# Attention and a Mish layer on one core: Mish written in bf16 steps with one reciprocal for eight denominators, and the exponential's VectorE share raised to 50 sets at a constant pace

## The chip, the cores and the metric

One Trainium2 chip, of which the program uses one core. The metric is the time of one execution in device microseconds (us). Three runs of the kernel before took 901.83, 902.10 and 903.09 us; their median is 902.1 us. In this text PE or TensorE is the matrix engine, ACT or ScalarE the engine of activations, DVE or VectorE the vector engine, POOL or GpSimd the fourth compute engine, SP the queue that issues most transfers.

## The reference

Two branches on the same input `x` (2048 rows of 640, bf16) are mixed by a gate per row:

```python
g = sigmoid((x * gate_w).sum(-1))                    # one gate per row
qkv = x @ wqkv                                       # 32 heads of 20 columns each
p = softmax(q @ k.T * 20**-0.5)                      # per head, 2048 x 2048
a = (p @ v) @ wo
h = x @ w1 + b1                                      # 2048 x 1536
sp = log1p(exp(-abs(h))) + max(h, 0)
b = (h * tanh(sp)) @ w2                              # Mish, then the second matrix
out = g * a + (1 - g) * b
```

With n = e^h (e^h + 2), Mish is h * n / (n + 2); the kernel computes it so. The softmax has 32 x 2048 x 2048 exponentials, 1,048,576 in each of the 128 partitions.

## The kernel before

**Attention.** The heads are taken four at a time (a "pair" `p`, 0 to 7; the name is the code's) and the queries 512 at a time (`qc`, 0 to 3). A (p, qc) is a *group*; there are 32. A group has 16 *sets*, one for each 128 keys, and a set has four *blocks*, one per head: 128 keys x 512 queries of scores. L1150 multiplies `kT` (32 rows of each of the four heads) by `qT` into a PSUM tile `Sp`; L1165 takes the exponential of a whole tile into `E`; L1225 multiplies `E` by the values `VA`, four heads beside each other, into the accumulator `acc`. The values carry a column of ones, so a row of `acc` is the softmax's sum. At the end of a group `normalise` (L1180 to L1211, all on VectorE) turns `acc` round (L1185), inverts the sums, scales, and turns it back into a 128x512 `cell` (L1202).

The score tiles alternate between three blocks (tag S0) and two blocks (tag S1), one buffer each, so scores of iteration i+2 need the tile of iteration i back. One *iteration* is one tile. There are 819.

**The exponential on two engines.** Some sets go to VectorE. In an iteration with a three-block tile, ACT then reads only two blocks, and VectorE reads the third (L794 in `jv_read`) into one slot of `E_dve` (a ring of three buffers). After four such reads a set is complete, and seven further steps (L810 to L832 in `jv_steps`) work the exponential out in integer and fp16 arithmetic, 2048 elements per partition each. L1225 then uses it with `VB`, a scaled copy of the values. `JV_SETS` says how many sets of a group are VectorE's, `JV_START` and `blocks` at which point of the run (in groups) each read is due: groups 1 to 31 have one and two sets in turn, 47 in all, and the reads of group G begin 0.9 of a group before it (other offsets for groups 1, 25 and 32).

**The Mish branch.** `h_chain` multiplies `x` by `w1` (L660), VectorE adds the bias (L670); for each pair of 512-wide pieces `mish_steps` (L579 to L645) issues one ACT exponential into a float32 tile `e` (L589) and then eleven VectorE instructions. Before, these are, each on 1024 elements unless said otherwise: n (L596, float32 to float32), the clip and + 2 (L599, float32 to fp16 `d`), products of two denominators (L603, 512, float32 out), of four (L608, 256), two reciprocals (L609, 128 each), back to two (L612, 512), back to one (L618), n times the inverse (L626, with float32 input), and two products with h (L632, 512 each). `b_chain` multiplies the result by `w2` (L693), scales it by 1 - g (L705).

**The end.** The first six pairs' cells go to memory and come back when a query chunk's turn comes (`fetch`); pairs 6 and 7 keep theirs. When a query chunk has all eight, `wo_chain` multiplies by `wo` (L739), and L756 adds the two branches and stores the rows. For the last chunk this is done without pair 7 into `R`; the very end adds pair 7's part (L1408, L1421).

**What orders the work.** The program is written out by hand, in one order per engine, by a planner in the kernel's own code. It keeps a clock per engine (`T`) with a cost for each instruction. `pump` puts pieces of projection, Mish and output matmuls (the chains, with start and due iteration) between an iteration's scores and the next; where nothing is due it puts in a filling multiplication of a constant tile (L1090), to keep TensorE active. `steps` and `run_slow` place the VectorE steps of the Mish pairs, the seven steps of a set and the rest of `normalise` into the gaps that VectorE's clock has before the next read. `wo_sb` is cleared by eight VectorE memsets (L1350) during group 16, before its load.

An iteration with a three-block tile gets a read by VectorE when the next one is due:

```python
x = None
far = G + (pos - unit_at[(G, 0)]) / (4.0 * (NS - JV_SETS.get(G, 0)))
if n == 3 and blocks and blocks[0][0] <= far:
    ...
    n = 2
```

Of the kernel before, what the change touches and what calls it, by code (L numbers as in the profile page):

```python
# [2 lines left out]

# [147 lines left out]
def kernel(  # L151
# [12 lines left out]
    nc = tc.nc  # L164
# [8 lines left out]
    QC = 512  # L173
    NQC = S // QC
    NU = QC // P
    NQ = H // 4
# [2 lines left out]
    Q_SCALE = 512.0 * float(DH) ** -0.5 / LN2  # L179
    WIDTHS = (3, 2)  # L180

    JV_TWO = (*range(2, 31, 2), 31)
    JV_SETS = {G: 2 if G in JV_TWO else 1 for G in range(1, 32)}
    JV_RING = 3
    JV_AHEAD = 0.9
    JV_BIAS = 32
    N_CAP = 16382.0
    NCELL = 40
    MLP_FROM, MLP_TO = 10, 1
    CELLS_KEPT = 2  # L190

# [111 lines left out]


    groups = [(p, qc) for p in range(NQ - 2) for qc in range(NQC)]
    groups += [(p, qc) for qc in range(NQC) for p in (NQ - 2, NQ - 1)]
    first = {}
    for G, (p, qc) in enumerate(groups):
        first.setdefault(p, G)


    units = []
# [6 lines left out]
    JV_START = {G: G - JV_AHEAD for G in range(34)}  # L319
    JV_START.update({1: 0.95, 25: 24.85, 32: 31.1})  # L320
    blocks = deque(
        (JV_START[G] + b * min(1.0, JV_START[G + 1] - JV_START[G]) / n, G, k, c)
        for G in JV_SETS
        for n in (4 * JV_SETS[G],)
        for b, (k, c) in enumerate((k, c) for k in range(JV_SETS[G]) for c in range(4))
    )
# [32 lines left out]
    def it_at(G, j=0):  # L359
        return it_of[unit_at[(G, j)]] if G < len(groups) else NI  # L360
# [218 lines left out]
    def mish_steps(m, c):  # L579


        h = h_of.pop((m, c))
        mish_free[0] = False
        e = mp.tile([P, 2 * QC], F32, tag="e", name="e")
        d = mp.tile([P, 4, 2 * P], F16, tag="d", name="d")
        d2 = mp.tile([P, 2, 2 * P], F32, tag="d2", name="d2")
        d4 = mp.tile([P, 2 * P], F32, tag="d4", name="d4")
# [4 lines left out]
        r = d2.rearrange("p a n -> p (a n)").bitcast(F16)  # L592
        y = d.rearrange("p a n -> p (a n)").bitcast(BF16)

        def n():
            V.scalar_tensor_tensor(out=e, in0=e, scalar=2.0, in1=e, op0=ALU.add, op1=ALU.mult)  # L596

        def products():
            V.tensor_scalar(  # L599
                out=d.rearrange("p a n -> p (a n)"), in0=e, scalar1=N_CAP, scalar2=2.0,  # L600
                op0=ALU.min, op1=ALU.add,
            )
            V.tensor_tensor(out=d2, in0=d[:, 0:2, :], in1=d[:, 2:4, :], op=ALU.mult)  # L603

        def invert(half):
            cols = slice(half * P, (half + 1) * P)
            if half == 0:
                V.tensor_tensor(out=d4, in0=d2[:, 0, :], in1=d2[:, 1, :], op=ALU.mult)  # L608
            V.reciprocal(out=d4[:, cols], in_=d4[:, cols])  # L609

        def of_two():
            V.tensor_tensor(  # L612
                out=r2, in0=d2[:, ::-1, :], in1=d4.unsqueeze(1).to_broadcast([P, 2, 2 * P]),
                op=ALU.mult,
            )

        def of_one():
            V.tensor_tensor(  # L618
                out=r.rearrange("p (b a n) -> p b a n", b=2, a=2),
                in0=d.rearrange("p (b a) n -> p b a n", b=2)[:, ::-1, :, :],  # L620
                in1=r2.unsqueeze(1).to_broadcast([P, 2, 2, 2 * P]),
                op=ALU.mult,
            )

        def share():
            V.scalar_tensor_tensor(out=y, in0=e, scalar=N_CAP, in1=r, op0=ALU.min, op1=ALU.mult)  # L626
            mish_free[0] = True

        def last(half):
            ft = 2 * m + half  # L630
            t = taken.pop((ft, c))
            V.tensor_tensor(out=t, in0=h[:, half, :], in1=y[:, half * QC : (half + 1) * QC], op=ALU.mult)  # L632
# [771 lines left out]
    for u in range(NU):  # L1404
        s = NU * last_qc + u
        ps = spool.tile([P, 2, QC], F32, tag=f"S{u % 2}", name="po")
        for half in range(2):
            nc.tensor.matmul(  # L1408
                ps[:, half, 0:HALF],
                lhsT=OT[(NQ - 1, last_qc)][:, u * P : (u + 1) * P],  # L1410
                rhs=wo_sb[0][:, NQ - 1, half * HALF : (half + 1) * HALF],
                start=True,
                stop=True,
            )
        if u == 0:
            pair = mp.tile([P, 2, 2 * QC], BF16, tag="e", name="ot")
        if u < 2:
            ot = pair[:, u, :]
        else:
            ot = mp.tile([P, 2 * QC], BF16, tag=("d", "d2")[u - 2], name="ot")  # L1420
# [50 lines left out]
```

## Time and profile before

| | |
|---|---|
| median of three runs | 902.1 us |
| the profiled execution's own time | 902.6 us |
| its span, first to last instruction | 900.8 us |
| ACT busy | 878.0 us in 849 instructions |
| PE busy | 820.8 us |
| VectorE busy | 794.3 us in 1207 instructions |
| POOL busy | 25.3 us |
| first and last exponential of a score tile begin at | 10.7 us and 887.5 us |
| mean granted TensorE clock | 0.996 |

"Busy" counts the time in which an engine has at least one instruction's record open. On ACT and VectorE the records of neighbours overlap by a little under a tenth of a microsecond, so the sum of all records is larger than busy. A row of the table of groups gives line, engine, operation, tiles and shape, the number of instructions, busy us, mean ns of one record, and the idle time of the engine before it with what ended that.

### The profile page before, as it was taken

How to read it: one execution, taken by the hardware profiler on the slowest of the kernel's cores; microseconds unless marked ns; L12 is line 12 of the kernel's file. 1: busy time of each engine (PE TensorE's matmuls, PEld its weight loads, DVE VectorE, ACT ScalarE, POOL GpSimd, SP SyncE). 2: the span in 40 equal slices, each digit the busy share in tenths (PEclk: the TensorE clock that was granted, in tenths of full speed). 3: DMA queues.
4: the chain of work that ended last, by engine and by line, in shares of the span. 5: the costliest groups of instructions: out<-in, count | busy, mean ns of one | idle time of the engine just before them, and what ended most of it. 6: DMA issues, size and time to landing. Idle time of an engine off the chain costs nothing.

```text
span 900.8 us, 14880 instructions
## 1 busy us (share of the span) xinstructions
PE 820.8 (91%) x5993; PEld 297.1 (33%) x6081; DVE 794.3 (88%) x1207; ACT 878.0 (97%) x849; POOL 25.3 (3%) x39
## 2 busy tenths in 40 slices
PE   8999898999998998989999989998999988999996
PEld 4443333233333333333333332333333333333332
DVE  4499999989989999989998999999999999988784
ACT  6999999999999999999999999999999999999994
POOL 5000010000000000000100000000000000000000
PEclk9999999999999999999999999999999999999998
DMA  9100010001000001000102000100001001110111
GB/s 264 36 7 22 21 31 1 21 22 31 7 21 15 21 7 30 22 19 32 31 28 51 8 21 15 31 36 21 21 16 43 27 1 40 44 44 8 50 53 39
DMA packets 37730, 28.27 MB, mean 31 GB/s; under 512 B 10984, under 2 KB 36472, under 8 KB 37656
## 3 DMA queue, kind: packets, MB, share of 16 engines
q1 hardware_dynamic: 34968, 20.90, 8.0%
q0 software_dynamic: 1456, 5.62, 2.1%
q8 instruction: 48, 0.79, 0.4%
q10 hardware_dynamic: 1232, 0.76, 0.3%
q14 instruction: 26, 0.21, 0.1%
HBM read 18.88 MB, written 8.39 MB: 30 GB/s over the span
## 4 chain that ended last, share of the span: by engine, by line
ACT 70%; PE 17%; issue 11%; DVE 2%; DMA 0%; ACTq 0%
ACT E L1165 67%; PE Sp L1150 5%; PE acc L1225 3%; ACT e L589 2%; PE ps L739 2%; PE ps L693 2%; PE ps L522 1%; PE ps L550 1%; PE ps L879 1%; DVE ot L1421 0%; DMA xs<-in_A_x_dram 0%; PE ps L660 0%; PE ps L480 0%; PE ps L1090 0%; PE ps L1301 0%
## 5 line engine op out<-in xcount | busy, mean ns | idle before, releaser
L1165 ACT ACTIVATE E<-Sp 128x1024 bf16<-128x1024 f32 (+1 forms) x819 | 856.6, 1232 | 3.9 <-PE Sp L1150 1.9
L1150 PE MATMUL Sp<-qT,kT 32*128 32x512 bf16 x2048 | 323.0, 382 | 61.5 <-ACT E L1165 44.7
L1150 PEld LDWEIGHTS <-kT 32*128 32x128 bf16 x2048 | 108.2, 91 | 284.6 <-issue 234.4
L1225 PE MATMUL acc<-E,VA 128*21 128x512 bf16 x1860 | 183.8, 386 | 0.0
L794 DVE TENSOR_SCALAR E_dve<-Sp 128x512 int16<-128x512 f32 x188 | 128.7, 685 | 31.7 <-PE Sp L1150 29.9
L1225 PEld LDWEIGHTS <-VA 128*21 128x21 bf16 x1860 | 45.6, 88 | 102.6 <-issue 102.4
L693 PE MATMUL ps<-w_sb,cell 128*128 128x320 bf16 x384 | 76.0, 303 | 0.2 <-issue 0.2
L1090 PE MATMUL ps<-busy 128*128 128x512 bf16 x229 | 71.2, 384 | 1.8 <-issue 1.6
L660 PE MATMUL ps<-xT,w1t 128*128 128x512 bf16 x215 | 71.2, 385 | 1.3 <-issue 1.3
L829 DVE TENSOR_TENSOR w_dve<-w_dve,u_dve 128x2048 bf16<-128x2048 f16 x47 | 57.1, 1215 | 0.2
L832 DVE TENSOR_TENSOR E_dve<-E_dve,w_dve 128x2048 int16<-128x2048 int16 x47 | 57.1, 1215 | 0.2
L820 DVE TENSOR_TENSOR w_dve<-w_dve 128x2048 f16<-128x2048 f16 x47 | 56.9, 1211 | 0.0
L739 PE MATMUL ps<-wo_sb,cell 128*128 128x320 bf16 x248 | 47.9, 302 | 0.0
L522 PE MATMUL ps<-xT,wkp 128*128 128x512 bf16 x135 | 43.3, 384 | 2.4 <-issue 1.4
L522 PE MATMUL ps<-xT,wqp 128*128 128x512 bf16 x137 | 43.9, 384 | 1.1 <-issue 0.9
L609 DVE RECIPROCAL d<-d 128x128 f32<-128x128 f32 x48 | 43.8, 934 | 0.8
L693 PEld LDWEIGHTS <-cell 128*128 128x128 bf16 x384 | 29.1, 97 | 35.4 <-issue 29.5
L670 DVE TENSOR_SCALAR h<-ps,b1f 128x512 bf16<-128x512 f32 x48 | 35.1, 731 | 0.8 <-PE ps L660 0.5
L810 DVE TENSOR_SCALAR w_dve<-E_dve 128x2048 int16<-128x2048 int16 x47 | 32.5, 692 | 1.2
L550 PE MATMUL ps<-wv,xT 128*128 128x80 bf16 (+2 forms) x240 | 33.3, 258 | 0.3 <-DVE xT L488 0.3
L815 DVE TENSOR_SCALAR E_dve<-E_dve 128x2048 int16<-128x2048 int16 x47 | 32.2, 686 | 1.1
L826 DVE TENSOR_SCALAR w_dve<-w_dve 128x2048 f16<-128x2048 f16 x47 | 32.1, 684 | 0.8
(105 smaller groups left out, 608.0 us busy)
## 6 DMA issues: line engine op xcount, KB each, us to landing
w1t<-in_B_w_dram SPq DMA_DIRECT2D x22, 320.0 KB, 3.1
heads_dram<-cell SPq DMA_DIRECT2D x24, 128.0 KB, 1.7
cell<-heads_dram SPq DMA_DIRECT2D x24, 128.0 KB, 2.9
b_dram<-Bt SPq DMA_DIRECT2D x4, 640.0 KB, 3.2
out_dram<-ot SPq DMA_DIRECT2D x14, 160.0 KB, 1.8
xs<-in_A_x_dram POOLq DMA_DIRECT2D x3, 640.0 KB, 7.1
w_sb<-in_B_w_dram POOLq DMA_DIRECT2D x1, 1920.0 KB, 12.6
ws<-in_A_wqkv_dram SPq DMA_DIRECT2D x13, 100.0 KB, 3.0
```

What stands on the lines that cost most here:

```text
L522: nc.tensor.matmul(box["ps"][:, :], lhsT=wpad[:, kt, :, :].rearrange("p h d -> p (h d)"), rhs=xT[:, kt, chunk * QC : (chunk + 1) * QC], st ...
L660: nc.tensor.matmul(box["ps"][:, :], lhsT=w1t[NPAIR * c + m][:, kt, half * P : (half + 1) * P], rhs=xT[:, kt, c * QC : (c + 1) * QC], start ...
L693: nc.tensor.matmul(box["ps"][:, :], lhsT=act[(ft, c)][:, u * P : (u + 1) * P], rhs=w2_sb[:, ft, half * HALF : (half + 1) * HALF], start=(f ...
L739: nc.tensor.matmul(box["ps"][:, :], lhsT=OT[(p, c)][:, u * P : (u + 1) * P], rhs=wo_sb[0][:, p, cols], start=(k == 0), stop=(k == len(ps_l ...
L794: S_reader[0] = nc.vector.tensor_scalar(out=E_dve[ring].bitcast(I16)[:, slot, :], in0=ps, scalar1=ROUND, scalar2=ROUND - 512.0 * JV_BIAS, ...
L820: V.tensor_tensor(out=w, in0=w, in1=w, op=ALU.mult)
L829: V.tensor_tensor(out=w.bitcast(BF16), in0=w, in1=u, op=ALU.mult)
L832: V.tensor_tensor(out=e, in0=e, in1=wi, op=ALU.add)
L1090: nc.tensor.matmul(ps[:, 0:n], lhsT=busy[:, :], rhs=busy_row(n), start=True, stop=True)
L1150: nc.tensor.matmul(ps[:, k * QC : (k + 1) * QC], lhsT=kT[p][32 * t : 32 * t + 32, j * P : (j + 1) * P], rhs=qT[G][32 * t : 32 * t + 32, :] ...
L1165: exp = nc.scalar.activation(E[:, 0 : n * QC], S_of.pop(i)[:, 0 : n * QC], ACT.Exp, scale=LN2 / 512.0)
L1225: nc.tensor.matmul(acc[32 * t : 32 * t + DH + 1, :], lhsT=v, rhs=e, start=(n == 0), stop=(n == NS - 1), tile_position=(0, 32 * t),)
```

## The change

Four edits, which leave the result's formula as it is.

1. **Mish.** n is written as bf16 (`y`), and the clip and the + 2 become two instructions on 16-bit data. The products are those of two, four and eight denominators; one reciprocal of 128 elements takes the place of two, and one more step leads from it back to four. The inverse lies in the first half of `e`, the products of eight and the inverses of four in its second half. The last product n times the inverse has two 16-bit inputs. Thirteen VectorE instructions in place of eleven. The planner's costs of the steps are changed with them. `N_CAP` is 16384 in place of 16382, and `y`'s memory is made up by two fewer cells (38 for 40).
2. **The VectorE share.** 50 sets in place of 47. The reads are due at a constant pace, one set per 0.603 of a group from 0.95 to 31.1; a set belongs to the group in which it is complete (up to 0.25 of a group later). Groups 2 to 31 have one or two, group 1 has none.
3. **The order of the last groups.** (6,0) (6,1) (7,0) (7,1), then as before (6,2) (7,2) (6,3) (7,3); before it was (6,0) (7,0) (6,1) (7,1). The keys of pair 7 are still projected during group 24; they are due five iterations later.
4. **The clearing of `wo_sb`** is POOL's in place of VectorE's.

```diff
-    JV_TWO = (*range(2, 31, 2), 31)
-    JV_SETS = {G: 2 if G in JV_TWO else 1 for G in range(1, 32)}
+    JV_N, JV_FROM, JV_TO, JV_LATE = 50, 0.95, 31.1, 0.25
-    JV_AHEAD = 0.9
-    N_CAP = 16382.0
-    NCELL = 40
+    N_CAP = 16384.0
+    NCELL = 38
...
-    groups += [(p, qc) for qc in range(NQC) for p in (NQ - 2, NQ - 1)]
+    groups += [(NQ - 2, 0), (NQ - 2, 1), (NQ - 1, 0), (NQ - 1, 1)]
+    groups += [(p, qc) for qc in range(2, NQC) for p in (NQ - 2, NQ - 1)]
...
+    set_length = (JV_TO - JV_FROM) / JV_N
+    JV_SETS = {}
+    blocks = deque()
+    for n in range(JV_N):
+        t = JV_FROM + n * set_length
+        G = min(max(1, math.ceil(t + set_length - JV_LATE)), len(groups) - 1)
+        k = JV_SETS.get(G, 0)
+        JV_SETS[G] = k + 1
+        t = max(t, G - 1.0)
+        blocks.extend((t + c * set_length / 4, G, k, c) for c in range(4))
...
         def n():
-            V.scalar_tensor_tensor(out=e, in0=e, scalar=2.0, in1=e, op0=ALU.add, op1=ALU.mult)
+            V.scalar_tensor_tensor(out=y, in0=e, scalar=2.0, in1=e, op0=ALU.add, op1=ALU.mult)
+        def bound():
+            V.tensor_scalar(out=y, in0=y, scalar1=N_CAP, scalar2=None, op0=ALU.min)
+        def denominator():
+            V.tensor_scalar(
+                out=d.rearrange("p a n -> p (a n)"), in0=y, scalar1=2.0, scalar2=None, op0=ALU.add
+            )
...
+        def of_eight():
+            V.tensor_tensor(out=d8, in0=d4[:, 0, :], in1=d4[:, 1, :], op=ALU.mult)
+        def invert():
+            V.reciprocal(out=d8, in_=d8)
+        def one_of_four():
+            V.tensor_tensor(
+                out=r4.rearrange("p (a n) -> p a n", a=2), in0=d4[:, ::-1, :],
+                in1=d8.unsqueeze(1).to_broadcast([P, 2, P]), op=ALU.mult,
+            )
...
         def share():
-            V.scalar_tensor_tensor(out=y, in0=e, scalar=N_CAP, in1=r, op0=ALU.min, op1=ALU.mult)
+            V.tensor_tensor(out=y, in0=y, in1=r, op=ALU.mult)
...
-                (1217, n, True), (1415, products, True), (1400, lambda: invert(0), True),
-                (947, lambda: invert(1), False), (692, of_two, True), (692, of_one, True),
-                (1222, share, True), (420, lambda: last(0), True), (420, lambda: last(1), False),
+                (1217, n, True), (427, bound, True), (427, denominator, True), (419, of_two, True),
+                (417, of_four, True), (292, of_eight, True), (947, invert, True),
+                (417, one_of_four, True), (692, one_of_two, True), (692, one, True),
+                (692, share, True), (420, lambda: last(0), True), (420, lambda: last(1), False),
...
         if p == NQ - 1:
-            a, b = it_at(first[p] - 1) + 1, it_at(first[p]) - 4
+            a = it_at(first[p - 1]) + 1
...
-        vec(330)
-        nc.vector.memset(wo_sb[0][:, p, :], 0.0)
+        nc.gpsimd.memset(wo_sb[0][:, p, :], 0.0)
```

More of the change, by code (lines that the diff above doesn't have):

```diff
@@ L1 @@
+import math
 from collections import deque
@@ L309 @@
         first.setdefault(p, G)
+    set_length = (JV_TO - JV_FROM) / JV_N
[8 more added lines that the diff above has]
+        blocks.extend((t + c * set_length / 4, G, k, c) for c in range(4))
+    assert max(JV_SETS.values()) <= 2
     units = []
@@ L318 @@
             units.extend((G, groups[G][0], groups[G][1], j, (j + k) % 4) for k in range(4))
[L319 to L326, printed above, removed]
     heads_of = {(G, k): [] for G in JV_SETS for k in range(JV_SETS[G])}
@@ L584, in mish_steps @@
         e = mp.tile([P, 2 * QC], F32, tag="e", name="e")
+        y = mp.tile([P, 2 * QC], BF16, tag="y", name="y")
         d = mp.tile([P, 4, 2 * P], F16, tag="d", name="d")
-        d2 = mp.tile([P, 2, 2 * P], F32, tag="d2", name="d2")
-        d4 = mp.tile([P, 2 * P], F32, tag="d4", name="d4")
+        d2 = mp.tile([P, 2, 2 * P], BF16, tag="d2", name="d2")
+        d4 = mp.tile([P, 2, P], F32, tag="d4", name="d4")
         r2 = mp.tile([P, 2, 2 * P], BF16, tag="r2", name="r2")
@@ L591, in mish_steps, with of_two, of_four, one_of_two @@
         V = nc.vector
-        r = d2.rearrange("p a n -> p (a n)").bitcast(F16)
-        y = d.rearrange("p a n -> p (a n)").bitcast(BF16)
+        r = e.bitcast(F16)[:, 0 : 2 * QC]
+        r4 = e[:, QC : QC + 2 * P]
+        d8 = e[:, QC + 2 * P : QC + 3 * P]
         def n():
-            V.scalar_tensor_tensor(out=e, in0=e, scalar=2.0, in1=e, op0=ALU.add, op1=ALU.mult)
-        def products():
+            V.scalar_tensor_tensor(out=y, in0=e, scalar=2.0, in1=e, op0=ALU.add, op1=ALU.mult)
+        def bound():
+            V.tensor_scalar(out=y, in0=y, scalar1=N_CAP, scalar2=None, op0=ALU.min)
+        def denominator():
             V.tensor_scalar(
-                out=d.rearrange("p a n -> p (a n)"), in0=e, scalar1=N_CAP, scalar2=2.0,
-                op0=ALU.min, op1=ALU.add,
+                out=d.rearrange("p a n -> p (a n)"), in0=y, scalar1=2.0, scalar2=None, op0=ALU.add
             )
+        def of_two():
             V.tensor_tensor(out=d2, in0=d[:, 0:2, :], in1=d[:, 2:4, :], op=ALU.mult)
[L605 to L611, printed above, removed]
+        def of_four():
             V.tensor_tensor(
-                out=r2, in0=d2[:, ::-1, :], in1=d4.unsqueeze(1).to_broadcast([P, 2, 2 * P]),
-                op=ALU.mult,
-            )
-        def of_one():
+                out=d4.rearrange("p a n -> p (a n)"), in0=d2[:, 0, :], in1=d2[:, 1, :], op=ALU.mult
+            )
+        def of_eight():
[7 more added lines that the diff above has]
+            )
+        def one_of_two():
+            V.tensor_tensor(
+                out=r2, in0=d2[:, ::-1, :],
+                in1=r4.unsqueeze(1).to_broadcast([P, 2, 2 * P]), op=ALU.mult,
+            )
+        def one():
             V.tensor_tensor(
@@ L1419 @@
         else:
-            ot = mp.tile([P, 2 * QC], BF16, tag=("d", "d2")[u - 2], name="ot")
+            ot = mp.tile([P, 2 * QC], BF16, tag=("d", "y")[u - 2], name="ot")
         nc.vector.scalar_tensor_tensor(
```

## The prediction

> **What bounds the kernel now.** I read the page first: busy times, the chain of work that ended last, the costliest groups.
>
> ```profile
> PE 820.8 (91%) x5993; PEld 297.1 (33%) x6081; DVE 794.3 (88%) x1207; ACT 878.0 (97%) x849; POOL 25.3 (3%) x39
> ...
> ACT 70%; PE 17%; issue 11%; DVE 2%; DMA 0%; ACTq 0%
> ...
> L1165 ACT ACTIVATE E<-Sp 128x1024 bf16<-128x1024 f32 (+1 forms) x819 | 856.6, 1232 | 3.9 <-PE Sp L1150 1.9
> ```
>
> ACT is busy 97% of the span and carries 70% of the chain; of the span 10.7 us lie ahead of the first exponential and 12 behind the last. In between ACT stands idle 3.9 us before its 819 exponentials. So what leaves ACT leaves the time, as long as nothing else becomes late. The groups with shapes kept apart give the price:
>
> ```profile
> L1165 ACT ACTIVATE E<-Sp 128x1024 bf16<-128x1024 f32 x597 | 597.4, 1116 | 2.9 <-PE Sp L1150 1.0 <-PE acc L1225 0.3 <-ACT E L1165 0.2
> L1165 ACT ACTIVATE E<-Sp 128x1536 bf16<-128x1536 f32 x222 | 342.5, 1543 | 1.0 <-PE Sp L1150 0.8
> ```
>
> The reader is to see 1543 - 1116 = 427 ns for a third block. These records overlap; by their starts one after another in the trace, the closest successor of a two-block exponential begins 0.903 us later, of a three-block one 1.330 us (the same 0.427 apart), and of a Mish exponential 0.947 us. I call the sum of these steps ACT's need. It is 597 x 0.903 + 222 x 1.330 + 24 x 0.947 = 857.1 us, against 878 us of real time: 20 us are lost in small waits. The table of stretches shows where:
>
> ```profile
> 240.00:268.00 28.00, 25.34 (x188) 9.49 (x187) 24.68 (x38) 28.00 (x28) 0.00 (x0) 1.00 0.08 22
> ...
> 324.00:352.00 28.00, 25.41 (x180) 8.55 (x181) 27.21 (x40) 28.00 (x29) 0.00 (x0) 1.00 0.10 24
> ...
> 800.00:828.00 28.00, 27.95 (x214) 10.58 (x211) 22.87 (x35) 27.67 (x27) 0.00 (x0) 1.00 0.08 25
> 828.00:856.00 28.00, 28.00 (x217) 10.24 (x216) 21.08 (x33) 27.11 (x27) 0.00 (x0) 1.00 0.12 42
> ```
>
> Columns: stretch, its length, then busy us of PE, PEld, DVE, ACT, POOL, then clock and DMA. In the middle ACT is full, also where VectorE is busy 27.21 of 28 us. From 800 us on it is not: there TensorE is full. What TensorE needs is read from its timeline near the end:
>
> ```profile
> 884.90 0.40 PE L1225 MATMUL acc<-E,VA 128*21 128x512 bf16 x4
> 885.23 0.85 PE L739 MATMUL ps<-wo_sb,cell 128*128 128x320 bf16 x5
> 886.01 0.39 PE L1150 MATMUL Sp<-qT,kT 32*128 32x512 bf16 x2
> 886.33 0.40 PE L1225 MATMUL acc<-E,VA 128*21 128x512 bf16 x4
> 886.66 0.45 PE L739 MATMUL ps<-wo_sb,cell 128*128 128x320 bf16 x2
> 887.04 0.39 PE L1150 MATMUL Sp<-qT,kT 32*128 32x512 bf16 x3
> ```
>
> From start to start: a tile of scores 0.32 us, a set of `acc` 0.33, five output matmuls 0.78, two 0.38; so 0.135 for each and 0.1 per burst.
>
> **ACT's share, exact.** Three more sets are 12 blocks that ACT does not read: 609 two-block and 210 three-block exponentials in the changed instruction list, 819 in all as before. 12 x 0.427 = **-5.1 us** of need. But it matters where they leave, and what bounds there. I counted each engine's instructions by iteration, before and after, in three stretches.
>
> *Iterations 0 to 64* (10.7 to 81.9 us, 71.2 us). Two- and three-block exponentials go from 46 and 19 to 42 and 23, as group 1 loses its set: ACT's need rises from 67.8 to 69.5 us. TensorE's need there, priced as above (the first projections and `x`'s Gram matrices fall here), is 69.4 us before and 69.5 after. So TensorE was already near the real pace, and half of ACT's +1.7 is hidden: between 0 and +1.7, I take **+0.9**.
>
> *Iterations 65 to 740* (81.9 to 803.6 us). 495 and 181 become 512 and 164: 17 x 0.427 = **-7.3 us**. Real time is 721.7 against a need of 709.5, so 12.2 us of small waits; TensorE needs only 575 us and its fillings. I leave these 12.2 us as they are, for the reasons under VectorE.
>
> *Iterations 741 to the end.* With (7,0) one group later, the output matmuls of query chunk 0 start a group later: by group 26 to 31 the list has 24, 36, 28, 30, 52, 78 of them before and 0, 26, 38, 46, 49, 89 after. In this stretch that makes 17 more 320-column matmuls (254 to 271, with `w2`'s), one more set, two more bursts: 17 x 0.135 + 0.33 + 0.2 = 2.8 us more on the engine that is full. ACT needs 79.8 before and 80.3 after, TensorE 85.7 and 88.5. Of the first 65 iterations here the real time was 69.7 at a TensorE need of 67.6 and 0.6 of filling, so 1.4 above; after it is 70.4 + 1.4 = 71.8; the last 13 iterations are alike. **+2.1 us**, between 0 and +2.8.
>
> **VectorE.** Rows for the Mish steps:
>
> ```profile
> L599 DVE TENSOR_SCALAR d<-e 128x1024 f16<-128x1024 f32 x24 | 16.7, 694 | 0.1
> ...
> L618 DVE TENSOR_TENSOR d<-d,r 128x1024 f16<-128x1024 f16 x24 | 16.5, 686 | 0.4
> ...
> L632 DVE TENSOR_TENSOR cell<-h,d 128x512 bf16<-128x512 bf16 x48 | 18.6, 416 | 0.5
> ...
> L299 DVE COPY wqp<-ws 128x400 bf16<-128x400 bf16 x1 | 0.3, 258 | 0.0
> ```
>
> Before: 1218 + 694 + 693 + 420 + 2 x 934 + 687 + 686 + 1216 + 2 x 416 = 8314 ns a pair. After: n 1218, as only its output shrinks. The clip and the + 2 on 1024 16-bit elements have no row: bounds are 258 (400 elements, L299) and 1218 (L596, the slowest on 1024); between L299 and the 16-bit steps of a set (2048 elements, 684 to 692) a straight line gives 420 each, which I take. Products of two 416 (L632), of four 420 (L608), of eight 284 (L603 and L608 carried on to 128 elements), the reciprocal 934, back to four 420, to two 687, to one 686, the share 686 (L618, also 16-bit in and out), 2 x 416: 7423 ns. Saved: 24 x 0.89 = 21.4 us. Three sets cost 3 x (4 x 685 + 6389) = 27.4 us (L794, L810 to L832), the memsets give back 8 x 0.325 = 2.6. That is +3.4 us of records in 73 more instructions. Neighbours that do not depend on each other overlap by about 0.085 us in the timeline, and the number of instructions that need the one directly before them is the same in both lists (258). So 73 x 0.085 = 6.2 us come back: VectorE's load is unchanged within 3 us, at nothing in the time; ACT's work is the cover. Were that cover gone, the 12 added reads would each hold a score tile. The waits of the reads show how near that is:
>
> ```profile
> PEld L1150 <- DVE E_dve L794: 15.7, 44, 0.8
> ```
>
> 44 of 188 reads made the next scores wait, 0.36 us each, and most of it ended inside ACT's cover. Counting the list from a set's fourth read to the place of its matmul, the changed order leaves VectorE 3.2 us or so more than its work in between, as before, so sets arrive in time.
>
> **POOL's memsets.** one L1341 took 0.84 us on POOL and its twin, beside VectorE's L832 and L810, 2.21 us, and L599 took 0.87 us in place of 0.69 beside a POOL copy at 600.2 us: the two engines do disturb each other. By POOL's 204 ns for 128 elements and 98 ns for one, 640 elements take some 0.63 us. Eight that each hold VectorE wholly are 5.1 us, or 2.5 more than the memsets they replace; by the L599 row 8 x 0.18 = 1.5, less than they replace. I take 0, and +2.5 as the bound. The queue behind them on POOL holds only the padding copies for pairs 5 to 7, which waited for TensorE 323 us in total. The Trainium skill, SBUF — State Buffer, section "Who interferes with whom", says that the pair of ports the two share is locked for a whole instruction by whoever starts first; the two rows agree in kind. By it the sum would be 2.5 us higher at worst, in group 16.
>
> **Sum.** +0.9 - 7.3 + 2.1 = -4.3 us. The profiled execution, 902.6 us, would become 898.3; it lies 0.5 above the median, so the median goes from 902.1 to **897.8 us**.
>
> **Rivals.**
> - *The two TensorE ends take more* (start +1.7, end +2.8, with POOL's 2.5 or without): -2.8 to -0.3, 899.3 to 901.8. For it: both ends are where TensorE is the bound. Against: the real time moved with the need there, not above it. Chance 0.14.
> - *The even pace also takes waits away.* The 12.2 us of the middle shrink by a fifth, since no group has its reads crowded: -2.4, 895.4. For it: reads stood in bunches before. Against: ACT is 28.00 of 28 in stretches of either kind. Chance 0.14.
> - *Slower: reads come late.* VectorE in the middle is 92% busy and is asked for more steps, each of which may stand in front of a read; a late read keeps the three-block tile, the next scores wait, then ACT. If the 12.2 us double: 897.8 + 12.2 = 910.0. It beats the saving once they grow by more than 4.3 us, a third. The two bf16 steps at their upper bound, 48 x 0.8 = 38 us that the planner has not counted, would do it. Against: the 324 row, 27.21 us of VectorE and no ACT idle. Chance 0.10.
> - That ACT's work does not shrink is excluded by the list of instructions.
>
> **Numbers.** Forecast 0.62 (896 to 899.3). A measurement of this kernel tells about 0.2% (1.8 us) from no change: below 900.3 is faster, above 903.9 slower. Faster: the forecast, the larger gain and 0.06 of the ends' rival, 0.82; same: the other 0.08 of it and 0.02 of the late reads, 0.10; slower: the rest of the late reads, 0.08. The range goes from 895.2 to 901.5, which leaves the late reads, the ends' worst and a larger gain outside.
>
> **What would show it.** ACT: 609 and 210 exponentials, a need of 852.0 us, and the L1165 row near 852 busy. Mish: the two 16-bit steps at 0.42 us, the reciprocal once, VectorE's busy time within 5 us of 794. TensorE full already from about 790 us. The wait of L1150's loads for the reads at 20 us or less. Wrong would be: ACT below 27.5 of 28 us in stretches between 90 and 770 us, or bf16 steps of 0.7 us and more.

## The result and the profile after

The changed kernel takes **904.9 us** (median of twelve runs, 903.55 to 906.18) beside 902.6 us (twelve runs, 901.83 to 904.19) for the kernel before: a ratio of 1.0024, with an interval of 1.0015 to 1.0033. It is slower by 2.4 us where 4.3 us of gain were forecast, and lies outside the range. The profiled execution took 904.87 us, with a span of 903.1 us. From here on lines are those of the changed kernel, 22 higher in the part that matters: L1187 is the exponential, L1172 the scores, L1247 `acc`, L816 VectorE's read, L832 the first of a set's seven steps.

The page of the changed kernel, in the order in which the page of before was read:

```profile
PE 832.8 (92%) x6070; PEld 291.2 (32%) x6070; DVE 794.0 (88%) x1280; ACT 874.8 (97%) x849; POOL 30.5 (3%) x47
...
ACT 58%; PE 24%; issue 9%; DVE 8%; DMA 0%; ACTq 0%
...
L1187 ACT ACTIVATE E<-Sp 128x1024 bf16<-128x1024 f32 (+1 forms) x819 | 853.1, 1219 | 7.2 <-PE acc L1247 3.0
```

ACT has lost 3.2 us of busy time (878.0 before), VectorE's busy time is as it was (794.3 before). But VectorE now carries 8% of the chain where it carried 2%, and ACT's idle time before its exponentials has gone from 3.9 to 7.2 us. The groups with shapes kept apart:

```profile
L1187 ACT ACTIVATE E<-Sp 128x1024 bf16<-128x1024 f32 x609 | 606.0, 1112 | 6.2 <-PE acc L1247 3.0 <-PE Sp L1172 0.7
...
L1187 ACT ACTIVATE E<-Sp 128x1536 bf16<-128x1536 f32 x210 | 321.0, 1529 | 1.0 <-PE Sp L1172 0.8
...
L832 DVE TENSOR_SCALAR w_dve<-E_dve 128x2048 int16<-128x2048 int16 x50 | 37.4, 748 | 0.8
```

The 609 and 210 exponentials are there. The third row holds the first sign of the cause: this step took 692 ns before, and its mean is now 748, 56 ns x 50 = 2.8 us in total. One instruction has all of it. The timelines of POOL and of VectorE, with start, length, engine, line, and in brackets the idle time ahead of it and its releaser:

```profile
437.14 4.63 POOL L1371 MEMSET wo_sb<- 128x640 bf16 x8
```

```profile
437.80 0.69 DVE L816 TENSOR_SCALAR E_dve<-Sp 128x512 int16<-128x512 f32 x1 [1.44 <-PE Sp L1172]
438.53 3.79 DVE L832 TENSOR_SCALAR w_dve<-E_dve 128x2048 int16<-128x2048 int16 x1
442.24 0.73 DVE L692 TENSOR_SCALAR h<-ps,b1f 128x512 bf16<-128x512 f32 x1
442.90 0.68 DVE L816 TENSOR_SCALAR E_dve<-Sp 128x512 int16<-128x512 f32 x1
```

POOL's eight memsets came as one burst of 4.63 us, to 441.77. L816, which reads PSUM, ran beside them in its usual time. L832, which began inside the burst, ended 0.55 us after the burst did, so it did its work after the last memset. The chain of waits of the same execution goes through it:

```profile
437.80 0.70 DVE E_dve L816
438.50 0.02 issue
438.53 3.79 DVE w_dve L832
442.32 0.65 DVE h L692
442.98 0.61 DVE E_dve L816
443.58 0.05 issue
443.63 0.61 PE Sp L1172 x3
```

Behind L832 stood the bias of a Mish piece, for which ACT waited 2.05 us, and the next read of a score tile, for which TensorE's scores waited 2.83 us. What came after cost nearly as much again. The granted clock of TensorE was at half from 443.4 to 446.8 us. Two rows of its timeline, the stretch (length, busy us of PE, PEld, DVE, ACT, POOL, then the clock), and ACT's row:

```profile
443.63 0.61 PE L1172 MATMUL Sp<-qT,kT 32*128 32x512 bf16 x3 [2.83 <-DVE E_dve L816]
444.17 2.31 PE L682 MATMUL ps<-xT,w1t 128*128 128x512 bf16 x5
```

```profile
443.40:446.80 3.40, 3.17 (x9) 0.84 (x9) 1.74 (x4) 2.49 (x3) 0.00 (x0) 0.50 0.00 0
```

```profile
447.65 1.94 ACT L1187 ACTIVATE E<-Sp 128x1024 bf16<-128x1024 f32 x2 [1.76 <-PE acc L1247]
```

The same five L682 take 1.25 us in the run with chained memsets below, at clock 1.00. The next scores came late for it, and ACT stood a second time, for 1.76 us at 447.65. All twelve executions of the changed kernel have a mean clock of 0.990 to 0.993; in the four runs below that change only how `wo_sb` is cleared, and in which L832 is held for 1.0 us at most, none is under 0.995. That TensorE's standing idle is what lowered the clock is likely from the order of the two, but no run changes the one without the other.

The waits of the weight loads for the reads are the second sign: the longest is now 3.1 us (0.8 before).

```profile
PEld L1172 <- DVE E_dve L816: 24.3, 58, 3.1
```

Stretches of the changed kernel; columns as in the prediction (length, busy us of PE, PEld, DVE, ACT, POOL, clock, DMA share, GB/s):

```profile
240.00:268.00 28.00, 26.02 (x192) 8.59 (x191) 26.73 (x44) 28.00 (x28) 0.00 (x0) 1.00 0.06 18
...
436.00:464.00 28.00, 23.26 (x156) 7.73 (x156) 24.61 (x34) 24.18 (x25) 5.78 (x10) 0.94 0.10 20
...
800.00:828.00 28.00, 28.00 (x222) 10.59 (x220) 21.51 (x35) 27.63 (x26) 0.00 (x0) 1.00 0.14 42
```

ACT is full at 240 us and limited by TensorE from 800 us on, as before. At 436 us 3.8 us are missing from ACT.

The same need of ACT as in the prediction (0.903, 1.330 and 0.947 us for a two-block, three-block and Mish exponential) beside real time, both in us, by stretches of iterations:

| iterations | before: real / need | after: real / need | change, forecast | change, measured |
|---|---|---|---|---|
| 0 to 64 | 71.2 / 67.8 | 72.4 / 69.5 | +0.9 | +1.2 |
| 65 to 740 | 721.7 / 709.5 | 721.1 / 702.2 | -7.3 | **-0.6** |
| of these 390 to 415 | 27.56 / 26.99 | 30.94 / 26.56 | | +3.4 |
| 741 to the start of the last | 83.85 / 78.5 | 85.15 / 78.9 | +2.1 | +1.3 |

The first exponential and the end behind the last one are each 0.2 us later. So the need of the middle fell by 7.3 us as forecast, and waits took 6.6 of it back. In iterations 390 to 415, where the burst lies, real time over need grew from 0.6 to 4.4, by 3.8 us; in the rest of the middle it grew from 11.6 to 14.4, by 2.8. These are the two things to test.

### The profile page after: what moved, and what is told of

The parts are those of the page before. It is cut to its first block, busy times and chain, and to the rows that moved or that the text cites. A ratio compares the mean times of both kernels' runs of the same rounds, so it can differ in the third digit from the quotient of the medians.

```text
span 903.1 us, 15020 instructions
## 1 busy us (share of the span) xinstructions
PE 832.8 (92%) x6070; PEld 291.2 (32%) x6070; DVE 794.0 (88%) x1280; ACT 874.8 (97%) x849; POOL 30.5 (3%) x47
## 4 chain that ended last, share of the span: by engine, by line
ACT 58%; PE 24%; issue 9%; DVE 8%; DMA 0%; ACTq 0%
ACT E L1187 55%; PE Sp L1172 7%; PE acc L1247 4%; PE ps L761 4%; ACT e L594 2%; PE ps L526 2%; PE ps L715 2%; PE ps L682 1%; DVE E_dve L816 1%; DVE w_dve L832 1%; PE ps L554 1%; PE ps L901 1%; PE ps L1112 1%; DVE E_dve L854 1%; DVE w_dve L851 1%
## 5 line engine op out<-in xcount | busy, mean ns | idle before, releaser
L1187 ACT ACTIVATE E<-Sp 128x1024 bf16<-128x1024 f32 (+1 forms) x819 | 853.1, 1219 | 7.2 <-PE acc L1247 3.0
L1172 PE MATMUL Sp<-qT,kT 32*128 32x512 bf16 x2048 | 323.3, 382 | 58.1 <-ACT E L1187 42.2
L1172 PEld LDWEIGHTS <-kT 32*128 32x128 bf16 x2048 | 105.1, 91 | 296.8 <-issue 237.3
L1247 PE MATMUL acc<-E,VA 128*21 128x512 bf16 x1848 | 182.5, 386 | 0.3 <-DVE T L1207 0.2
L816 DVE TENSOR_SCALAR E_dve<-Sp 128x512 int16<-128x512 f32 x200 | 137.0, 685 | 34.2 <-PE Sp L1172 32.8
L1247 PEld LDWEIGHTS <-VA 128*21 128x21 bf16 x1848 | 45.5, 88 | 99.6 <-issue 99.3
L682 PE MATMUL ps<-xT,w1t 128*128 128x512 bf16 x240 | 77.2, 390 | 0.0
L1112 PE MATMUL ps<-busy 128*128 128x512 bf16 (+1 forms) x243 | 76.6, 383 | 0.0
L854 DVE TENSOR_TENSOR E_dve<-E_dve,w_dve 128x2048 int16<-128x2048 int16 x50 | 60.6, 1213 | 0.2
L842 DVE TENSOR_TENSOR w_dve<-w_dve 128x2048 f16<-128x2048 f16 x50 | 60.6, 1213 | 0.0
L526 PE MATMUL ps<-xT,wkp 128*128 128x512 bf16 x155 | 48.7, 384 | 0.8 <-DVE xT L492 0.8
L526 PE MATMUL ps<-xT,wqp 128*128 128x512 bf16 x155 | 49.5, 384 | 0.0
L692 DVE TENSOR_SCALAR h<-ps,b1f 128x512 bf16<-128x512 f32 x48 | 35.5, 739 | 3.5 <-PE ps L682 3.4
L832 DVE TENSOR_SCALAR w_dve<-E_dve 128x2048 int16<-128x2048 int16 x50 | 37.4, 748 | 0.8
L848 DVE TENSOR_SCALAR w_dve<-w_dve 128x2048 f16<-128x2048 f16 x50 | 34.5, 690 | 1.0
L837 DVE TENSOR_SCALAR E_dve<-E_dve 128x2048 int16<-128x2048 int16 x50 | 34.3, 686 | 0.7
L845 DVE TENSOR_SCALAR u_dve<-w_dve 128x2048 f16<-128x2048 f16 x50 | 34.2, 684 | 0.6
```

The source lines that it names most:

```text
L526: nc.tensor.matmul(box["ps"][:, :], lhsT=wpad[:, kt, :, :].rearrange("p h d -> p (h d)"), rhs=xT[:, kt, chunk * QC : (chunk + 1) * QC], st ...
L682: nc.tensor.matmul(box["ps"][:, :], lhsT=w1t[NPAIR * c + m][:, kt, half * P : (half + 1) * P], rhs=xT[:, kt, c * QC : (c + 1) * QC], start ...
L816: S_reader[0] = nc.vector.tensor_scalar(out=E_dve[ring].bitcast(I16)[:, slot, :], in0=ps, scalar1=ROUND, scalar2=ROUND - 512.0 * JV_BIAS, ...
L842: V.tensor_tensor(out=w, in0=w, in1=w, op=ALU.mult)
L854: V.tensor_tensor(out=e, in0=e, in1=wi, op=ALU.add)
L1112: nc.tensor.matmul(ps[:, 0:n], lhsT=busy[:, :], rhs=busy_row(n), start=True, stop=True)
```

## The experiments

**Who clears `wo_sb`.** Theory: one instruction of VectorE is held until the whole burst is over, and this costs 4 us. Rival: the new steps and the even pace are what is late, and the burst only moves time about. The changed kernel with the clearing as it was before:

```diff
-        nc.gpsimd.memset(wo_sb[0][:, p, :], 0.0)
+        vec(330)
+        nc.vector.memset(wo_sb[0][:, p, :], 0.0)
```

> The changed kernel with edit 4 undone: wo_sb is cleared by VectorE again. Theory (the burst): eight memsets back to back on POOL kept VectorE's L832 open for 3.79 us in place of 0.69, the next reads and scores were late and ACT lost 3.8 us between iterations 390 and 416; without them L832 is 0.69 to 0.75 us each time, ACT stands at 27.5 or more of 28 us there, and the time is 904.9 - 3.8 = 901.1 us. Rival (the pace): VectorE is simply too full with 50 sets, the stall moves to another place, and the time stays at 904 us or above.

Measured 900.76 us (before 902.5 in the same runs), a ratio of 0.9981 (0.9972 to 0.9990). The theory holds: this one line is worth 4.1 us, by the medians against the kernel before. Iterations 390 to 415 take 26.96 us in place of 30.94, 4.0 less: 2.2 in the step across the Mish exponential that waited for L692, 1.8 in the step that ended late at half the clock. The stretch is whole again, the clock with it:

```profile
436.00:464.00 28.00, 24.90 (x178) 8.84 (x176) 25.00 (x42) 28.00 (x29) 0.72 (x2) 1.00 0.15 37
```

**The same line alone, in the kernel before** (POOL's memset in place of VectorE's, nothing else):

> The kernel before with edit 4 alone: wo_sb cleared by POOL. Theory (the burst): the memsets stand in POOL's queue behind the two scalings of VB and two copies here too, so they come as one burst of 4.6 us; one VectorE instruction on 16-bit data from one tensor is held for up to that long, ACT loses 2 to 4 us, 904.5 to 906.5 us. Rival (the pace): VectorE's 2.6 us of memsets go, nothing is held, 902 to 902.6 us.

Measured 902.55 us, 1.0005 (0.9995 to 1.0014). The expected loss did not come, although the burst did. Its timelines of POOL and of VectorE (lines of the kernel before, POOL's 1 lower):

```profile
432.86 4.64 POOL L1349 MEMSET wo_sb<- 128x640 bf16 x8
```

```profile
432.94 0.68 DVE L612 TENSOR_TENSOR r<-d,d 128x512 bf16<-128x512 f32 x1
433.65 0.69 DVE L618 TENSOR_TENSOR d<-d,r 128x1024 f16<-128x1024 f16 x1
434.77 0.69 DVE L794 TENSOR_SCALAR E_dve<-Sp 128x512 int16<-128x512 f32 x1 [0.42 <-PE Sp L1150]
435.39 0.69 DVE L533 TENSOR_SCALAR qT<-ps 128x512 bf16<-128x512 f32 x1
436.00 1.21 DVE L626 SCALAR_TENSOR_TENSOR d<-e,d 128x1024 bf16<-128x1024 f32 x1
```

The burst met only steps with two inputs in SBUF and steps that read PSUM, and all kept their usual lengths. The price is not that of a POOL memset but of what VectorE has to do in those 4.6 us: a step with one 16-bit input in SBUF, as L832, is held, these are not. The Trainium skill, SBUF — State Buffer, section "Who interferes with whom", says that steps in a mode that uses both pairs of ports, or with two inputs against a POOL instruction that reads, contend with POOL, and others do not. This run agrees as far as two-input steps beside memsets go, which read nothing; that L832 works in such a mode is not seen in any trace.

**The burst, longer and shorter.** Each memset issued twice, or each as half as many elements of 32 bits:

```diff
         nc.gpsimd.memset(wo_sb[0][:, p, :], 0.0)
+        nc.gpsimd.memset(wo_sb[0][:, p, :], 0.0)
```

> The changed kernel with every memset of wo_sb issued twice on POOL, 16 in one burst. Theory (a burst keeps VectorE's instruction out until its end): the burst lasts 9.2 us in place of 4.6, the L832 that meets it is open for about 8.4 us in place of 3.79, ACT loses 4.6 us more: 909.5 us. Rival (VectorE gets in between two memsets, and the 3.79 us had another cause): L832 stays below 4 us, 905 to 906 us.

```diff
-        nc.gpsimd.memset(wo_sb[0][:, p, :], 0.0)
+        nc.gpsimd.memset(wo_sb[0][:, p, :].bitcast(mybir.dt.uint32), 0)
```

> The changed kernel with POOL's memsets written as 320 elements of 4 bytes in place of 640 of 2, the same bytes. Theory (the burst's length is the price): a memset takes about 0.37 us in place of 0.63, the burst 2.7 in place of 4.6, L832 about 1.9 in place of 3.79, so 1.9 us come back: 903.0 us. Rival (any burst there costs the same, as one late step is enough): 904.5 us or more.

Twice the memsets gave 900.11 us, 0.9971 (0.9961 to 0.9981): faster than the changed kernel by 4.8 us, where 4.6 more had been expected. The timelines of POOL and of VectorE in it:

```profile
437.18 0.63 POOL L1371 MEMSET wo_sb<- 128x640 bf16 x1
437.87 0.63 POOL L1372 MEMSET wo_sb<- 128x640 bf16 x1
438.44 0.63 POOL L1371 MEMSET wo_sb<- 128x640 bf16 x1
439.12 1.06 POOL L1372 MEMSET wo_sb<- 128x640 bf16 x1
```

```profile
438.57 1.04 DVE L832 TENSOR_SCALAR w_dve<-E_dve 128x2048 int16<-128x2048 int16 x1
```

A second memset on the same memory waits for the first, so there is a gap of 0.06 us between 437.81 and 437.87 and again ahead of 439.12. L832 began at 438.57, inside the third memset, and was done 0.54 us after that one's end at 439.07. Now it is the fourth memset that is held (1.06 in place of 0.63). So VectorE does not wait for POOL to have nothing to do; it can get in between two instructions. At a gap it did. But the same run shows that a gap is not the only way in (POOL's and VectorE's timelines):

```profile
440.81 0.63 POOL L1372 MEMSET wo_sb<- 128x640 bf16 x1
441.38 1.17 POOL L1371 MEMSET wo_sb<- 128x640 bf16 x1
```

```profile
440.79 1.20 DVE L837 TENSOR_SCALAR E_dve<-E_dve 128x2048 int16<-128x2048 int16 x1
```

L837 (0.68 us otherwise) was held by the memset of 440.81 and done 0.55 us after its end at 441.44. Yet the memset of 441.38 waits for nothing and there is no gap ahead of it; it was the one held, 1.17 us. The same happens to L848 at 445.78. In the burst of eight, L832 got in at none of the five such boundaries that it met. One difference in the records: L837 and L848 were issued within 0.04 us of the start of the memset that held them, L832 in the middle of one. Whether that decides was not tested. What is shown is that with a wait before every second memset no VectorE step was held for longer than one of them.

The 32-bit form nearly halved the burst, and cut L832's delay from 3.1 to 1.0 us (columns as above, POOL's and VectorE's timelines):

```profile
436.76 2.50 POOL L1371 MEMSET wo_sb<- 128x320 uint32 x8
```

```profile
438.14 1.66 DVE L832 TENSOR_SCALAR w_dve<-E_dve 128x2048 int16<-128x2048 int16 x1
```

L832 again ended 0.54 us after the burst, and its length is near the 1.9 us that had been expected; the time, 900.91 us, 0.9976 (0.9967 to 0.9986), is 2 us better than expected. So the delay is not paid one for one: 1.0 us of it (1.66 - 0.69) costs next to nothing (900.91 beside 900.76 for no burst; 27.33 beside 26.96 us in iterations 390 to 415), 3.1 us cost 4. Two things lie between, by the traces: the read stood some way ahead of the scores that needed it, so that the first part of the delay was hidden (TensorE waited 0.69 us here, 2.83 there); and the clock stayed at 1.00 here, while 1.8 of the 4 us there were lost in the stretch at half the clock.

**A gap by design.** Each memset of POOL also clears the last two columns of the one before it, and so waits for it:

```diff
-        nc.gpsimd.memset(wo_sb[0][:, p, :], 0.0)
+        flat = wo_sb[0][:, :, :].rearrange("p q c -> p (q c)")
+        nc.gpsimd.memset(flat[:, max(0, p * D - 2) : (p + 1) * D], 0.0)
```

> The changed kernel with POOL's eight memsets kept, but each also clears the last two columns of the one before it, so that each waits for the end of that one, as every second one did when they were issued twice. Theory (a burst without gaps keeps VectorE's instruction out, a gap of some 0.06 us lets it in): the L832 or other 16-bit step that meets the memsets is held for one memset at most, 0.7 to 1.4 us in place of 3.79, and the time is 900 to 901 us. Rival (VectorE was let in by chance when they were issued twice): L832 is held to the end of the burst again, 903 us or more.

```profile
436.79 6.36 POOL L1372 MEMSET wo_sb<- 128x640 bf16 x8
```

```profile
438.17 1.17 DVE L832 TENSOR_SCALAR w_dve<-E_dve 128x2048 int16<-128x2048 int16 x1
```

Measured **899.73 us**, 0.9956 (0.9943 to 0.9969), the lowest median of all that ran and faster than both kernels; its interval overlaps that of the memsets issued twice, so these two are not told apart. POOL takes longer for its eight memsets (6.36 us for 4.63), and L832 waits for one of them. As all boundaries have a gap here, the run does not settle what let L837 in above; it shows that the expected remedy works.

**Mish alone**, in the kernel before (edit 1, nothing else):

> The kernel before with edit 1 alone: Mish in bf16 steps, 47 sets. ACT's need is unchanged, VectorE is asked for some 17 us less. Theory (VectorE's load is covered by ACT): 902.2 to 902.8 us, no change. Rival (the small waits of the middle follow VectorE's load): they shrink, 901.5 us or less. The two 16-bit steps take 0.42 us each, the products of eight 0.28.

901.91 us, 0.9992 (0.9983 to 1.0001), at 771.9 us of VectorE's busy time (794.3 before): 22 us less of VectorE's work change nothing that can be told. At 47 sets ACT's work covers it. The other way round, the changed kernel with the old Mish at 50 sets (clearing by VectorE):

> 50 sets at the constant pace, the new order and clearing by VectorE, but Mish as before, in eleven steps with two reciprocals, which is 17 us more for VectorE. Theory (VectorE's load decides how late reads are): the time over ACT's need after read tiles rises from 8.9 to 12 us or more, 903 to 906 us: Mish's new form is what pays for the three sets. Rival (the load is covered by ACT): 900.5 to 901.5 us, as with the new Mish.

941.05 us, 1.0419 (1.0397 to 1.0441). The Mish work no longer finds room among the reads: its last three exponentials begin at 831, 876 and 896 us (705, 731 and 762 with the new Mish). What waits for them, the products with `w2` and the last output matmuls, runs behind the last scores, when ACT has hardly anything left:

```profile
892.00:920.00 28.00, 19.37 (x121) 11.46 (x120) 16.69 (x26) 3.98 (x4) 0.00 (x0) 0.82 0.00 1
```

Expected had been 903 to 906 us. So edit 1 is worth nothing by itself and about 40 us as the room that edit 2 needs with this planner. "At nothing in the time" was right for a VectorE load that stays as it was, but the cover ends within the 21 us that edit 1 saves.

**The sets and the order of groups, taken apart.** The changed kernel, clearing by VectorE, with the old order of the last groups:

```diff
-    groups += [(NQ - 2, 0), (NQ - 2, 1), (NQ - 1, 0), (NQ - 1, 1)]
-    groups += [(p, qc) for qc in range(2, NQC) for p in (NQ - 2, NQ - 1)]
+    groups += [(p, qc) for qc in range(NQC) for p in (NQ - 2, NQ - 1)]
...
-        t = max(t, G - 1.0)
+        t = max(t, 24.85 if G == 25 else G - 1.0)
...
-            a = it_at(first[p - 1]) + 1
+            a, b = it_at(first[p] - 1) + 1, it_at(first[p]) - 4
```

> Mish in bf16 steps and 50 sets alone: clearing by VectorE and the old order of the last groups, with the reads of group 25 not before 24.85 as in the kernel before. Theory (the end is TensorE's): the 1.7 us that iterations 728 to the end took more go, 901.1 - 1.7 = 899.4 us, and TensorE's need after iteration 741 is back at about 86 us. Rival (the end is not set by the order): 900.8 us or more, within 0.3 us of the changed kernel with clearing by VectorE.

908.27 us, 1.0068 (1.0055 to 1.0082): 7.5 us worse than with the new order, where 1.4 better had been expected. The end is indeed cheaper (iterations 741 on: 84.4 us for 85.15), but ahead of it ACT loses more:

```profile
700.00:728.00 28.00, 23.00 (x159) 7.40 (x159) 24.43 (x35) 25.67 (x27) 0.00 (x0) 1.00 0.04 12
728.00:756.00 28.00, 25.09 (x177) 8.50 (x173) 26.43 (x45) 24.64 (x25) 0.00 (x0) 0.94 0.10 30
```

With the new order ACT has 28.00 and 27.77 there, at clock 1.00. With the old sets (47, in ones and twos), the new order and the new Mish:

> The changed kernel with clearing by VectorE and the 47 sets of before, one and two in turn: Mish in bf16 steps and the new order alone. ACT's need is 5.1 us more than with 50. Theory (late reads): the steps after a tile that VectorE reads, between 81 and 800 us, are 5 us over ACT's need in all, as before, in place of 8.9; with the end's TensorE surplus 902.5 to 904 us. Rival (the waits come from Mish's 13 shorter steps): they stay near 8 us and the time is 905 us or more.

908.35 us, 1.0055 (1.0036 to 1.0074), over 4 us above what had been expected; the loss is in nearly the same place:

```profile
728.00:756.00 28.00, 23.75 (x166) 8.04 (x169) 25.15 (x47) 26.47 (x26) 0.00 (x0) 0.98 0.00 1
756.00:784.00 28.00, 26.43 (x177) 8.51 (x177) 22.68 (x35) 25.85 (x26) 0.00 (x0) 0.90 0.11 36
```

And edit 3 alone in the kernel before (its two pieces as in the diff above, from the old to the new form):

> The kernel before with edit 3 alone, the new order of the last groups with the 47 sets of before. The prediction's step would make this +2.1 us, 904.6 us. Theory (order and pace belong together: groups 24 to 27 are crowded unless both are as before or both are new): 906 us or more, with ACT short of its need by over 4 us between 670 and 784 us. Rival (Mish's new form did the harm in the run with the old sets): 903 to 905 us.

906.71 us, 1.0041 (1.0027 to 1.0055). By the medians edits 2 and 3 belong together: either with the other's old form costs 4 to 8 us, both together do not. Where the time goes is less sure than that. In the traces of the first two runs, iterations 416 to 740 hold 6.4 and 4.6 us more waits than the kernel each is compared with (clearing by VectorE with the new order, and the kernel before), part of it at a clock that the rows above show at 0.94 and 0.90. The profiled execution of the third took 904.30 us, the fastest of its six; it has 1.7 us more there, ACT is busy 1.4 us less than before between 672 and 784 us, where over 4 had been expected, and the clock stays at 1.00. Its two executions with a mean clock of 0.996 took 904.3 and 904.5 us, the four at 0.991 to 0.993 took 906.4 to 907.9: so the new order alone costs about 2 us, and more in executions with a lower clock, which no trace of it shows. Which instruction is late there was not followed up.

**The even pace at 47 sets** (`JV_N = 47`, clearing by VectorE):

> As the one before, but with 47 sets at the constant pace, one per 0.641 of a group. ACT's need is that of 47 sets. Theory A (the pace makes reads late, whatever their number): 8 to 9 us over the need after read tiles, 904.5 to 906 us. Theory B (their number does, VectorE being nearly full): 5 to 6.5 us over, and the same time as with one and two in turn, within 0.7 us.

903.13 us, 1.0006 (0.9997 to 1.0015). The excess after read tiles is 6.7 us; the time lies below theory A's, and 5.2 us under that of one and two in turn, so neither theory holds as it was put. Real time over need in iterations 65 to 740 is 13.5 us (12.2 before, 15.3 at 50 sets): the even pace does not take waits away; with the new order and the new Mish, which this kernel has too, it adds 1.3 (the new Mish alone adds nothing, 12.0), and three more sets add 1.8.

**Where the small waits of the middle come from.** The part of them that grew sits after tiles that VectorE has read: the excess there between 81 and 800 us is 5.4 us before, 8.9 with 50 sets and no burst, some 55 ns a read for 35; elsewhere it is 6.8 and 6.4. In most of the late ones (18 of the 30 that were more than 0.1 us late with 50 sets) TensorE was still in another chain's or a filling 512-column multiplication when the scores could have begun; one waited for the read itself. Two guesses. First, that VectorE's other steps are put too close ahead of a read (clearing by VectorE):

```diff
-        run_slow(full + 100.0)
+        run_slow(full - 100.0)
```

> The changed kernel with clearing by VectorE, and the planner told to place no slow VectorE step that would end later than 0.1 us before the scores of the next read are there (it was 0.1 us after). Theory (late reads cost what the middle lacks): the time over ACT's need after read tiles between 81 and 800 us falls from 8.9 to about 6 us, the time from 900.8 to 898 us. Rival (VectorE has no room to leave idle): steps pile up, sets come late, 901.5 us or more.

900.85 us, 0.9966 (0.9953 to 0.9980), and the excess after read tiles is 9.4 us: no fall. Second, that TensorE's pieces end too late; its limit is set 0.1 us earlier, in the kernel with the chained memsets and in the kernel before:

```diff
-        limit = T["act"] + NS_EXP[iters[min(i + 1, NI - 1)][1]] - NS_SCORES_SEEN - 60.0
+        limit = T["act"] + NS_EXP[iters[min(i + 1, NI - 1)][1]] - NS_SCORES_SEEN - 160.0
```

> The changed kernel with the chained memsets on POOL, and pump told to stop 0.16 us, in place of 0.06, ahead of the time at which the next scores have to be issued. Theory (after a tile that VectorE reads ACT steps on after 0.903 us, and scores come late because TensorE is still in a projection or filling piece): the time over ACT's need after read tiles between 81 and 800 us falls from 9.2 to 5 to 7 us, and the time from 899.7 to 896 to 898. Rival (the scores wait for VectorE's reads): it stays at 9 us and the time at 899.5 or more.

> The kernel before with the same 0.16 us in place of 0.06. Theory as in the run before: the kernel before has 154 read tiles with 5.4 us over the need, so less to win, 900.5 to 902 us. Rival: no change, 902.5 us, or slower as pieces are put off to the end, where TensorE is full.

904.24 us, 1.0022 (1.0006 to 1.0038), with an excess of 8.5 us for 9.2 without it; and 902.86 us, 1.0002 (0.9994 to 1.0011), with 5.4 as before. The first guess is refuted. The second is not borne out, but not cleanly tested: by the medians the run is 4.5 us slower than without its edit, and its trace shows the clock at half from 173.3 to 180.1 us, where 2.4 us over the need are lost; outside the iterations there the excess after read tiles is 8.0 us for 9.2, a fall of 1.2 where 2 to 4 had been expected. The cause stays open. What is shown is only that these waits are larger with the even pace (beside the other edits) and with more reads.

## Why the prediction was wrong, step by step

- **POOL's memsets: the step that failed.** "I take 0, and +2.5 as the bound": the working saw that the two engines disturb each other, and it even had a row where POOL stood held beside the very step (L810, now L832). But it priced eight memsets as a sum of records and subtracted the memsets that they replace. Both halves were wrong. What is replaced costs nothing in the time, being covered by ACT (22 us less of VectorE's work changed nothing in the run with Mish alone), so it could not be subtracted. And the eight are one burst: behind two scalings that waited 154 us and two copies, nothing on POOL kept them apart, so one step waited for all that was left of it, 3.1 us, in front of a read for which TensorE and ACT stood. It cost 4.1 us by the medians, 4.0 in iterations 390 to 415: 2.2 of that is ACT's wait behind the held step, 1.8 were lost right after, while TensorE worked at half its clock, for which the sum had no term. What the prediction cites from the Trainium skill, SBUF — State Buffer, section "Who interferes with whom", that the lock holds for a whole instruction, fell short in the same way: by it L832 would be held for one memset, 0.6 us; the trace shows it held through the five that followed as well.
- **The small waits of the middle, mis-sized.** "I leave these 12.2 us as they are": they are 15.3 us with the burst taken out, +3.1. The rival of late reads named this direction and a size four times as large; its reason, a load that the planner had not counted, was not the cause, as the two 16-bit steps took what was forecast. What does cause them stays open.
- **ACT's share: right.** 12 blocks, 609 and 210 exponentials, -7.3 us of need in the middle. The two-block and three-block steps kept their pace: 1112 and 1529 ns a record for 1116 and 1543.
- **The start and the end: right in kind.** +1.2 for +0.9, inside its bounds; +1.3 for +2.1, inside its bounds.
- **VectorE's load: right in amount, and covered as long as it stays so.** Busy 794.0 us for 794.3 before; the durations taken from neighbouring rows (420 for the clip and the + 2, 416, 420 and 284 for the products) came out within 4%, as the rows below show.
- **The order of the groups** was priced as TensorE's work at the end only (+2.1). Alone it costs 4 us by the medians, of which its trace, of a faster execution, shows 1.7 ahead of the end and 0.5 at it; the even pace of the reads undoes what is ahead of the end. The prediction took the edits one by one and saw neither.

The added steps of Mish among the groups of the changed kernel, with their shapes apart:

```profile
L608 DVE TENSOR_SCALAR d<-y 128x1024 f16<-128x1024 bf16 x24 | 10.4, 431 | 0.5
L613 DVE TENSOR_TENSOR d<-d 128x512 bf16<-128x512 f16 x24 | 10.2, 425 | 0.5
...
L605 DVE TENSOR_SCALAR y<-y 128x1024 bf16<-128x1024 bf16 x24 | 10.0, 418 | 0.4
...
L621 DVE TENSOR_TENSOR e<-d 128x128 f32<-128x128 f32 x24 | 7.0, 293 | 0.5
```

L605 is the clip, L608 the + 2, L613 the products of two denominators, L621 those of eight.

By the medians the change gives 1.7 us with the burst gone, and with POOL clearing through gaps 2.8 to 3.5 (899.73 against 902.5 and against the 903.27 of its own runs), of the 4.3 forecast.

## What to carry to other kernels

An instruction moved to an idle engine is not free: look at what is queued ahead of it there, whether it will come as a burst without gaps, and which single instruction of the neighbour it can meet, for that one may wait for the rest of the burst, and everything behind it does too. A wait between the instructions of such a burst, here two overlapping columns, let the other engine in, at the price of a longer burst that nobody waits for. A stall long enough to leave TensorE idle can also cost more than its length: look at the granted clock behind it. And work that stands under a cover is worth nothing when it is removed, so it may not be set off against a cost that stands on the path.

## What the runs showed of the hardware

- Back-to-back POOL memsets kept a VectorE step on one 16-bit SBUF input out for the whole rest of the burst (3.79 us for 0.69); with gaps of 0.06 us between them it waited for one (1.04 and 1.17). The Trainium skill, SBUF — State Buffer, section "Who interferes with whom", speaks of one instruction; that an engine can lose again and again is what these runs add. A gap is not always needed: two steps got in at a boundary without one (1.20 and 1.08 us).
- VectorE steps with two SBUF inputs, and steps that read PSUM, ran beside the same burst in their usual time (0.68, 0.69 and 1.21 us).
- The loser can be POOL as well: a memset took 1.06 us for 0.63 beside L832.
- After TensorE had stood for 2.83 us, its granted clock was 0.50 for 3.4 us, and five 512-column multiplications took 2.31 us for 1.25; after 0.69 us of standing (the 32-bit run) it stayed at 1.00.
- A memset of 128x640 bf16 took POOL 0.63 us, the same bytes as 320 elements of 32 bits 0.36 us (eight in a burst 4.63 and 2.50 us).
